# The last block product accumulated on an earlier product's PSUM bank and written out in three parts

## The chip, the cores and the metric

The kernel runs on one core of a Trainium2 chip. The metric is the device time of one execution, in microseconds. A core has a matrix engine (TensorE, PE in the profile, with its weight loads shown as PEld), two engines that can read the matrix engine's result memory PSUM (VectorE, shown as DVE, and ScalarE, shown as ACT), GpSimd (POOL), and SyncE (SP), which here mostly starts DMAs. PSUM is handed out in banks of 512 fp32 values for each of 128 partitions.

## The reference

```python
# x [8, 8, 512, 64], state [8, 8, 32, 64], w_in [512, 2048], w_out [2048, 512]
scores = scale * x @ state.T;    xread = softmax(scores) @ state      # 512 rows per batch and head
scores2 = scale * state @ x.T;   sread = softmax(scores2) @ x         # 32 rows per batch and head
x2 = concatenate([xread, sread], axis=2), heads side by side: [8 * 544, 512]
h = x2 @ w_in
g = maximum(0.01 * h, h)
out = g @ w_out                                                       # [4352, 512] float32
```

## The kernel before

The eight batches go through attention and the first product one after the other. The first product leaves the activations of a batch, already passed through the leaky ReLU, as `hT`: 2048 hidden features on partitions, 512 rows. The second product (`hT` times `w_out`) of batches 2 to 7 is done by a scheme of Strassen's kind: the batch's rows, the hidden features and the output columns are each cut in two, and seven block products take the place of eight. The block products are numbered 1 to 7. Each has 256 output rows (two groups of 128, index `i` of the bank) and `HC` = 256 output columns, so one block product fills one PSUM bank `[P, 2, HC]`, and it is a sum over `NM` = 8 slices `m`. That makes 16 matmuls of 128x128 weights by 256 columns for a block product.

The block products are done in the order 1, 2, 6, 5, 7, 3, 4 on two banks: 1, 6, 7 and 4 share one, 2, 5 and 3 the other. 6 and 7 accumulate on what 1 left, 3 on what 5 left; 1, 2, 5 and 4 start afresh. `save` copies a bank to SBUF (1, 6, 5, 7, by ScalarE), and the four quarters of the output are then made by additions: `join` (line 569, DVE: bank plus a saved copy) and one addition of two saved copies by GpSimd (line 627). In steady state product 4 is such a `join` too: bank plus `sv[7]`, the saved state of its own bank after product 7.

Batch 7 is the last, and its second product is finished after the loop, between the pieces of a smaller product for the 256 rows of `sread` (tiles `hs`, `yhs`, banks `yu`). `before.run(9)` finishes product 7 of batch 7 with its `save`, the `sread` product follows, `before.run(8)` does product 3 and its `join`, and then the last loop of the kernel does product 4. There it is written out by hand: one group `i` of 128 rows at a time. The first group goes on the bank that held 1, 6 and 7 (`before.bank[7]`, shown as `yq`), the second on a bank of its own (`yz`). DVE adds the saved copy of product 7 to each (line 1090), and `before.out` (line 594) starts one DMA of 128 KB for each, the first on ScalarE's queue, the second on SyncE's.

The order of instructions on each engine is the order in which the program issues them. The waits between engines are put in by the framework, from the tiles that the instructions read and write. All matmuls of the block products are issued at line 557, in `unit`.

Of the kernel before, what the change touches and what calls it, by code (L numbers as in the profile page):

```python
# [9 lines left out]
P = 128  # L10
# [10 lines left out]
FP32 = mybir.dt.float32  # L21
AF = mybir.ActivationFunctionType
ALU = mybir.AluOpType
# [4 lines left out]
def kernel(  # L28
# [9 lines left out]
    nc = tc.nc  # L38
# [9 lines left out]
    psum = ctx.enter_context(tc.tile_pool(name="psum", bufs=2, space=bass.MemoryType.PSUM))  # L48
# [5 lines left out]
    VEC, SCA, POO = nc.vector.tensor_copy, nc.scalar.copy, nc.gpsimd.tensor_copy  # L54
# [452 lines left out]
    HC = DM // 2  # L507
# [17 lines left out]
    class Fast:  # L525
# [19 lines left out]
            with nc.allow_low_precision(reason="operands of a product"):  # L545
                (eng or nc.vector).tensor_tensor(out=S[n][:, ms], in0=u[:, ms], in1=v[:, ms], op=op)  # L546

        def unit(self, bank, n, m, first, of=None):
            A, S = self.A, self.S
            lhs = {1: A[1, 1], 2: A[1, 2], 4: A[2, 2]}.get(n)  # L550
            if lhs is None:
                lhs = S[{3: 3, 5: 0, 6: 1, 7: 2}[n]]
            rhs = {1: B11, 2: B21, 3: B22}.get(n)
            if rhs is None:
                rhs = tw[{4: 3, 5: 0, 6: 1, 7: 2}[n]]
            for i in range(self.sub) if of is None else (of,):
                nc.tensor.matmul(  # L557
                    bank[:, i, :], lhsT=lhs[:, m, P * i:P * (i + 1)], rhs=rhs[:, m, :],
                    start=(first and m == 0 and (i == 0 or of is not None)), stop=(m == NM - 1),
                    skip_group_check=True,  # L560
                )
# [139 lines left out]
    def max0(u):  # L701
        m = att.tile([P, NG], FP32, name="m0", tag="m0")
        nc.vector.tensor_reduce(out=m[:], in_=sct[u][:], axis=AX.X, op=ALU.max, negate=True)
        return m

    def split0(m):
        hi = att.tile([P, NG], BF16, name="hi0", tag="hi0")
        VEC(hi[:], m[:])
        lo = att.tile([P, NG], BF16, name="lo0", tag="lo0")
        with nc.allow_low_precision(reason="the second of two parts of one fp32 value"):  # L710
            nc.vector.tensor_tensor(out=lo[:], in0=m[:], in1=hi[:], op=ALU.subtract)
        return hi, lo
# [53 lines left out]
    m = max0(0)  # L766
    xt0_evict(1, pxt, (SCA, VEC))
    rows0(0)
    m = split0(m)
    scores0(1)  # L770
    m = m, max0(1)
# [124 lines left out]
    for s in range(16):  # L896
# [4 lines left out]
        if s % 2:  # L901
            pb, hT, i, jq = fill[s // 2]
# [27 lines left out]
    before = None  # L930
    weights_open()
    for b in range(2, B):
# [16 lines left out]
        for s in range(16):  # L949
# [70 lines left out]
            if std:  # L1020
                i, jq = std.pop(0)
# [11 lines left out]
        before = now  # L1033
# [33 lines left out]
    for n in (1, 2, 6, 5, 7, 3, 4):  # L1067
        bank = v if n in (2, 5, 3) else u
# [6 lines left out]
        elif n == 7:  # L1075
            nc.gpsimd.tensor_tensor(
                out=ysb[1][:, :, HC:], in0=fs.sv[7][:], in1=fs.sv[5][:], op=ALU.add
# [5 lines left out]
            fs.join(ysb[1][:, :, :HC], bank, 7)  # L1083
            out_s(1)
    before.run(8)
    for i in range(2):
        bank = before.bank[7] if i == 0 else psum.tile([P, 2, HC], FP32, name="yz", tag="big", bufs=1)[:]
        for m in range(NM):
            before.f.unit(bank, 4, m, first=True, of=i)
        nc.vector.tensor_tensor(  # L1090
            out=before.yo(1)[:, i, :HC], in0=bank[:, i, :], in1=before.f.sv[7][:, i, :], op=ALU.add
        )
        before.out(1, slice(0, HC), i, eng=(nc.scalar, nc.sync)[i])


# [28 lines left out]
```

## Time and the profile before

| what | us |
|---|---|
| median of three runs (lowest, highest) | 204.59 (204.48, 204.68) |
| profiled execution, its own time | 204.49 |
| its span, first to last instruction | 202.7 |
| PE busy in it | 197.0 (97%) |
| DVE busy | 151.4 (75%) |
| ACT busy | 143.7 (71%) |
| mean granted TensorE clock | 1.000 |

The span is the profiled execution without what lies around it; here 1.8 us of the execution's time lie outside the span. The busy time of PE counts a matmul from its start to its modelled end, and consecutive matmuls overlap, so a matmul shown as 273 ns may follow its predecessor by much less. The duration of a DMA's row is its issue; its landing is given apart.

### The profile page before, as it was taken

The numbers are of one execution on the slowest core, as the hardware profiler recorded it, in microseconds if no ns is written. First come the engines' busy times: TensorE is split into PE (matmuls) and PEld (weight loads), VectorE is DVE, ScalarE is ACT, GpSimd is POOL, SyncE is SP. The second block draws the span as 40 slices with busy tenths as digits, with TensorE's granted clock in tenths as the row PEclk, the third lists the DMA queues.
The fourth block names the chain that finished last, engine by engine and source line by source line (L and its number), as shares of the span: only waits on it lengthen the run. The fifth ranks groups of instructions, "written<-read, shape, count | busy, mean of one in ns | idle before, by whom it ended". The sixth has DMA issues, their size and how long they took to land.

```text
span 202.7 us, 4755 instructions
## 1 busy us (share of the span) xinstructions
PE 197.0 (97%) x1964; PEld 126.0 (62%) x1964; DVE 151.4 (75%) x230; ACT 143.7 (71%) x265; POOL 39.7 (20%) x66
## 2 busy tenths in 40 slices
PE   7899999999999999999999999999999999999993
PEld 2543544444344567766776767766767677799882
DVE  1677679599799969976996699769968853686612
ACT  3458848589869796978697878788778856467710
POOL 8831002021005005200251040200020002004250
PEclk9999999999999999999999999999999999999999
DMA  6999996999477895537946795250017100410035
GB/s 189 223 207 277 229 298 113 141 303 245 53 175 214 114 275 109 103 125 253 118 29 181 240 127 105 103 159 5 0 57 198 27 0 32 178 55 0 3 89 170
DMA packets 39733, 27.99 MB, mean 138 GB/s; under 512 B 25312, under 2 KB 36704, under 8 KB 39712
## 3 DMA queue, kind: packets, MB, share of 16 engines
q1 hardware_dynamic: 34512, 20.88, 44.6%
q0 software_dynamic: 4912, 6.55, 15.8%
q10 hardware_dynamic: 288, 0.26, 0.6%
q8 instruction: 15, 0.25, 0.5%
q14 instruction: 6, 0.05, 0.1%
HBM read 17.30 MB, written 8.91 MB: 129 GB/s over the span
## 4 chain that ended last, share of the span: by engine, by line
PE 96%; DVE 1%; ACT 1%; issue 0%
PE yq L557 36%; PE ph L372 23%; PE py L487 10%; PE pm L351 4%; PE pyw L487 3%; PE pf L441 3%; PE yu L557 3%; PE pspin L132 3%; PE ph L804 2%; PE sc L206 1%; PE psn L318 1%; PE phw L383 1%; PE php L804 1%; DVE M L365 1%; ACT xT L666 1%; PE scn L695 0%
## 5 line engine op out<-in xcount | busy, mean ns | idle before, releaser
L377 ACT ACTIVATE hT<-ph 128x512 bf16<-128x512 f32 x108 | 63.5, 604 | 22.0 <-PE ph L372 21.4
L372 PE MATMUL ph<-aT,M 128*128 128x512 bf16 x216 | 62.3, 379 | 0.0
L557 PEld LDWEIGHTS <-su 128*128 128x128 bf16 x416 | 39.7, 98 | 14.5 <-DVE su L546 1.7
L557 PEld LDWEIGHTS <-hT 128*128 128x128 bf16 x288 | 27.7, 98 | 11.7 <-issue 1.1
L557 PE MATMUL yq<-tw_xf,su 128*128 128x256 bf16 x192 | 27.2, 273 | 0.0
L105 POOL CAST xb<-xl 128x512 bf16<-128x512 f32 (+1 forms) x21 | 14.4, 724 | 65.2 <-PE ph L372 40.6
L557 PE MATMUL yq<-w_out_bf,hT 128*128 128x256 bf16 x192 | 27.0, 273 | 0.0
L372 PEld LDWEIGHTS <-M 128*128 128x128 bf16 x216 | 21.0, 98 | 9.3 <-issue 0.8
L546 DVE TENSOR_TENSOR su<-hT 128x1024 bf16<-128x1024 bf16 x24 | 16.8, 700 | 10.5 <-ACT hT L377 10.5
L487 PE MATMUL py<-w_out_bf,hT 128*128 128x512 bf16 x96 | 24.2, 379 | 0.0
L487 PEld LDWEIGHTS <-hT 128*128 128x128 bf16 x128 | 12.1, 98 | 14.6 <-issue 0.9
L627 POOL TENSOR_TENSOR yo<-sv,sv 128x512 f32<-128x512 f32 x6 | 7.8, 1300 | 54.1 <-ACT sv L566 42.7
L569 DVE TENSOR_TENSOR yo<-yq,sv 128x512 f32<-128x512 f32 x17 | 11.6, 685 | 6.5 <-PE yq L557 6.5
L566 ACT COPY sv<-yq 128x512 f32<-128x512 f32 x24 | 13.9, 585 | 2.0 <-PE yq L557 1.4
L365 ACT CAST M<-pm 128x1024 bf16<-128x1024 f32 x13 | 13.2, 1014 | 0.9 <-PE pm L351 0.8
L557 PE MATMUL yq<-w_out_bf,su 128*128 128x256 bf16 x96 | 13.1, 273 | 0.0
L557 PE MATMUL yq<-tw_x,su 128*128 128x256 bf16 x96 | 13.1, 272 | 0.0
L557 PE MATMUL yq<-tw_x,hT 128*128 128x256 bf16 x88 | 12.1, 273 | 0.0
L274 ACT ACTIVATE e<-sc,mcols 128x512 bf16<-128x512 f32 x16 | 11.1, 696 | 0.0
L216 DVE TRANSPOSE_TENSOR_REDUCE mrow<-sc 128x32 f32<-128x1024 f32 x7 | 8.7, 1245 | 2.4 <-PE sc L206 2.4
L266 DVE TENSOR_REDUCE mcol<-sc 128x2 f32<-128x1024 f32 x8 | 9.7, 1215 | 0.0
L247 DVE STREAM_TRANSPOSE qb<-qh 128x1024 bf16<-128x1024 bf16 x7 | 8.7, 1245 | 0.2
(147 smaller groups left out, 271.3 us busy)
## 6 DMA issues: line engine op xcount, KB each, us to landing
xl<-in_x_dram SPq DMA_DIRECT2D x5, 1024.0 KB, 7.1
out_dram<-yo SPq DMA_DIRECT2D x10, 512.0 KB, 3.0
w_in_bf<-in_moe_w_in_dram POOLq DMA_DIRECT2D x4, 512.0 KB, 9.1
w_out_bf<-in_moe_w_out_dram POOLq DMA_DIRECT2D x4, 512.0 KB, 17.0
out_dram<-ysb SPq DMA_DIRECT2D x8, 256.0 KB, 5.1
xf<-in_x_dram SPq DMA_DIRECT2D x2, 512.0 KB, 4.8
x<-in_x_dram POOLq DMA_DIRECT2D x2, 512.0 KB, 13.8
xl<-in_x_dram POOLq DMA_DIRECT2D x1, 1024.0 KB, 19.8
```

What stands on the lines that cost most here:

```text
L105: copy(xs[b][:, :, h0:h1].rearrange("p t h d -> p h t d"), xl[b][:, h0:h1].rearrange("p h (t d) -> p h t d", t=NT),)
L216: nc.vector.tensor_reduce(out=m1[:], in_=flat.rearrange("p (c j) -> p c j", j=NS), axis=AX.X, op=ALU.max, apply_transpose=True,)
L266: nc.vector.tensor_reduce(out=m2[:], in_=a.sc[:], axis=AX.X, op=ALU.max, negate=True)
L274: nc.scalar.activation(out=a.e2[:, g], in_=a.sc[:, g, :], func=AF.Exp, bias=a.m2s[:, g:g + 1], scale=SCALE, accum_out=a.r2[:, g:g + 1],)
L365: copy(a.M[:, :, cols], pm[:])
L372: nc.tensor.matmul(ph[:], lhsT=a.M[:, g, P * j:P * (j + 1)], rhs=a.aT[:, g, :], start=(g == 0), stop=(g == 1),)
L377: nc.scalar.activation(out=hT[:, j, :], in_=ph[:], func=AF.Prelu, alpha=0.01)
L487: nc.tensor.matmul(y.py, lhsT=hT[:, j, P * i:P * (i + 1)], rhs=w_out_bf[:, j, :], start=(j == 0), stop=(j == 15),)
L546: (eng or nc.vector).tensor_tensor(out=S[n][:, ms], in0=u[:, ms], in1=v[:, ms], op=op)
L557: nc.tensor.matmul(bank[:, i, :], lhsT=lhs[:, m, P * i:P * (i + 1)], rhs=rhs[:, m, :], start=(first and m == 0 and (i == 0 or of is not No ...
L566: copy(t[:], bank)
L569: nc.vector.tensor_tensor(out=dst, in0=bank, in1=self.sv[n][:], op=ALU.add)
```

## The change

Product 4 now starts from what product 7 left on the bank: its matmuls no longer carry `start`, so the sum that DVE made with the saved copy of product 7 is made by accumulation in PSUM. All of product 4 goes on that one bank; the bank `yz` is gone. The product is done in three parts in place of two: the first group of 128 rows with all 256 columns, then the second group's first 128 columns, then its last 128 columns. Each part is copied to SBUF as it stands, the first and third by DVE and the second by ScalarE, and each has its own output DMA: the first on SyncE's queue, the second on ScalarE's, the third on SyncE's.

```diff
-        def unit(self, bank, n, m, first, of=None):
+        def unit(self, bank, n, m, first, of=None, cols=slice(0, HC)):
...
-                    bank[:, i, :], lhsT=lhs[:, m, P * i:P * (i + 1)], rhs=rhs[:, m, :],
+                    bank[:, i, cols], lhsT=lhs[:, m, P * i:P * (i + 1)], rhs=rhs[:, m, cols],
                     start=(first and m == 0 and (i == 0 or of is not None)), stop=(m == NM - 1),
...
     before.run(8)
-    for i in range(2):
-        bank = before.bank[7] if i == 0 else psum.tile([P, 2, HC], FP32, name="yz", tag="big", bufs=1)[:]
+
+    bank = before.bank[7]
+    for i, cols, copy, eng in (
+        (0, slice(0, HC), VEC, nc.sync),
+        (1, slice(0, HC // 2), SCA, nc.scalar),
+        (1, slice(HC // 2, HC), VEC, nc.sync),
+    ):
         for m in range(NM):
-            before.f.unit(bank, 4, m, first=True, of=i)
-        nc.vector.tensor_tensor(
-            out=before.yo(1)[:, i, :HC], in0=bank[:, i, :], in1=before.f.sv[7][:, i, :], op=ALU.add
-        )
-        before.out(1, slice(0, HC), i, eng=(nc.scalar, nc.sync)[i])
+            before.f.unit(bank, 4, m, first=False, of=i, cols=cols)
+        copy(before.yo(1)[:, i, cols], bank[:, i, cols])
+        before.out(1, cols, i, eng=eng)
```

`VEC` is `nc.vector.tensor_copy` and `SCA` is `nc.scalar.copy`.

## The prediction

> **What bounds the kernel now.** I read the page first: how busy the engines are, and the chain that ended last.
>
> ```profile
> PE 197.0 (97%) x1964; PEld 126.0 (62%) x1964; DVE 151.4 (75%) x230; ACT 143.7 (71%) x265; POOL 39.7 (20%) x66
> ...
> PE 96%; DVE 1%; ACT 1%; issue 0%
> ```
>
> PE bounds the kernel: 96% of the chain. The change touches only the last 5 us, so I read those next, in the chain in order of time. There the columns are start, length, and what; the last row's x8 are eight matmuls.
>
> ```profile
> 186.35 0.45 PE pf L441 x8
> ...
> 195.76 2.62 PE yq L557 x24
> 198.38 0.89 PE yz L557 x8
> 199.26 0.02 issue
> 199.29 0.42 DVE yo L1090
> ```
>
> To the very end PE runs with no gap: 24 matmuls in 2.62 us is 0.109 us for one of 256 columns. (The pf row gives the price for 128 columns with weights of their own: 0.45/8 = 0.056 us.) Then only one addition is left, and its output. Third, the timeline of the same stretch shows who follows whom.
>
> ```profile
> 197.34 1.04 PE L557 MATMUL yq<-tw_x,hT 128*128 128x256 bf16 x8
> 197.54 0.69 DVE L569 TENSOR_TENSOR yo<-yq,sv 128x512 f32<-128x512 f32 x1 [1.25 <-PE yq L557]
> 198.21 1.04 PE L557 MATMUL yz<-tw_x,hT 128*128 128x256 bf16 x8
> 198.26 1.84 SPq L594 DMA_DIRECT2D out_dram<-yo  x2
> 198.47 0.42 DVE L1090 TENSOR_TENSOR yo<-yq,sv 128x256 f32<-128x256 f32 x1 [0.24 <-PE yq L557]
> 198.93 0.35 ACTq L594 DMA_DIRECT2D out_dram<-yo  x1
> 199.29 0.42 DVE L1090 TENSOR_TENSOR yo<-yz,sv 128x256 f32<-128x256 f32 x1 [0.39 <-PE yz L557]
> ```
>
> What matters is the overlap: DVE reads the first half from 198.47 to 198.89, and PE writes the second half from 198.21 to 199.25. They can, because yq and yz are two tiles on two banks. The last addition ends at 199.71, SyncE's second issue starts at 199.74, and the DMA view gives its landing.
>
> ```profile
> out_dram<-yhs SPq DMA_DIRECT2D x4, 64.0 KB, 1.9
> out_dram<-yo ACTq DMA_DIRECT2D x1, 128.0 KB, 2.2
> out_dram<-yo SPq DMA_DIRECT2D x1, 128.0 KB, 1.9
> ```
>
> So the last output lands near 201.6, and the span ends at 202.7: a fixed 1.1 us that the change doesn't touch.
>
> **The change part by part.** *Matmuls.* 16 of 256 columns become 8 of 256 and 16 of 128. By the rows above that is 16 x 0.109 = 1.75 us against 8 x 0.109 + 16 x 0.056 = 1.77: nothing. Accumulating in place of starting afresh changes no matmul's duration. Product 7 on that bank ended before the sread product, 189.64 at the latest, and its saved copy is still needed by GpSimd's addition (line 627), so no work ahead of 197.34 goes or moves.
>
> The Trainium skill, "TensorE: Matmul & The Clock Gate", section "Back-to-back issue gap", gives about 81 ns for a matmul of 128 columns in a stream of weight loads and matmuls. The pf row shows 56 ns for just that, so the measurement decides; by the page the sum below would be larger by 2 x 7 x 0.025 = 0.35 us.
>
> *Additions that become copies.* From the groups by shape:
>
> ```profile
> L465 DVE COPY sf<-pf 128x512 f32<-128x512 f32 x2 | 1.4, 692 | 0.0
> L1090 DVE TENSOR_TENSOR yo<-yq,sv 128x256 f32<-128x256 f32 x1 | 0.4, 425 | 0.2 <-PE yq L557 0.2
> L566 ACT COPY sv<-yu 128x256 f32<-128x256 f32 x4 | 1.5, 372 | 2.4 <-PE yu L557 2.4
> L326 ACT CAST sr_n<-psn 128x128 bf16<-128x128 f32 x1 | 0.3, 265 | 0.7 <-PE psn L318 0.7
> L441 PE MATMUL pf<-tx,sw 128*128 128x128 bf16 x48 | 3.7, 219 | 0.0
> ```
>
> A DVE copy out of PSUM at 512 columns takes 692 ns; the addition of 512 columns (line 569, first row of that line in the timeline) takes 0.69 too. So a copy is no cheaper than the addition, and at 256 columns I take 425. From (692 - 425)/256 = 1.04 ns a column, 128 columns are 425 - 133 = 0.29 us. That last copy is shorter by 0.13 than the addition it replaces: the only gain inside the chain. ScalarE's copy of 128 columns is 0.27 by its nearest row; ScalarE has nothing else to do by then.
>
> *The bank.* This is the term that decides. Parts 2 and 3 are written to the bank from which part 1 and part 2 are being read. The trace of before has no such case to price it: every tile is read only when all its matmuls are done, and where two halves are finished apart, as here, the second has a bank of its own. The bounds are nothing, if PE may write other columns of a bank while it is read, and the whole of each copy, if the framework makes a writer of a bank wait for earlier readers of it. I take the second: the program gives waits by the tile, the tile is now one, and it is one bank. Then PE, whose order is fixed, stops twice, with nothing queued behind that could fill in: part 2 waits for DVE's copy, part 3 for ScalarE's.
>
> The Trainium skill, "PSUM — Partial Sum Buffer", section "PSUM bank collisions raise a hardware error", says that TensorE writing and another engine reading one bank on the same 32 partitions at once is an error even at other columns, and asks for a guard by bank. No run here shows a collision; the rule speaks against this change, and by it the sum is the one below.
>
> The price of a restart is read early in the trace, where PE waited for a copy: DVE's xT copy ends at 6.68 + 0.42 = 7.10 and PE starts at 7.17; ScalarE's ends at 6.97 + 0.58 = 7.55 and PE starts at 7.61. So 0.06 or a little less; I take 0.05. The longest such row, at 74.42 + 0.69 = 75.11 to 75.25, is 0.14. A part of 128 columns takes 7 x 0.056 + 0.219 = 0.61 us from its first start to its last end.
>
> The sum, in order:
> - part 1 ends at 197.34 + 1.04 = 198.38 as before; DVE copies from 198.47 to 198.90
> - PE restarts at 198.95, part 2 ends at 199.56; ScalarE starts 0.04 later (as DVE after yz: 199.25 to 199.29), 199.60 to 199.87
> - PE restarts at 199.92, part 3 ends at 200.53; DVE copies from 200.57 to 200.86
> - SyncE issues 0.03 later (as before), at 200.89, against 199.74: 1.15 later.
>
> *The outputs.* SyncE's queue now carries part 1, behind the 256 KB output, at about 198.9, and is free again long before 200.89. ScalarE's issue at 199.90 lands by 2.2 us later at 202.1, ahead of the last one. The last output is 64 KB in place of 128. The rows of 64 KB on SyncE's queue land in 1.9 in the middle, and the quickest of them in 1.6; the change also leaves the DMA engines with less beside it. I take 1.75, so 0.15 less than before. It lands at 202.64 against 201.64: **1.0 us later**. On the profiled execution's own time that is 204.49 + 1.0 = 205.49; the median stands 0.10 above that execution, so I predict **205.6**.
>
> **The rivals.** *No stops* (not slower). PE runs on: the three parts follow without a gap and part 3 ends at 198.21 + 15 x 0.056 + 0.219 = 199.27, as before; DVE's shorter copy ends at 199.60 in place of 199.71, and the smaller output lands 0.15 sooner: 0.26 less, 204.3. It decides if part 2's first matmul starts before 198.47, ahead of DVE's copy. For it: the columns don't overlap. Against it: one tile, one bank.
>
> *One stop.* Only DVE's copy holds PE: part 3 ends at 198.95 + 15 x 0.056 + 0.219 = 200.01, 0.52 sooner than in the sum, so 205.1. Only ScalarE's holds it: part 2 starts at 198.21, its copy ends at 199.14, part 3 ends at 199.80, 0.73 sooner: 204.9. Nothing in the profile parts the two stops from each other.
>
> *Dearer stops.* Each restart costs 0.14 in place of 0.05 (+0.18), and the last output takes 1.9 or even 2.1 us, as the others of its size did (+0.15 to +0.35): up to 206.1. For it: the 75.25 row. Against it: those DMAs had others beside them. Cheaper ones: a copy that starts 0.04 after PE in place of 0.09, a landing in 1.64, and a copy of 128 columns at DVE's shortest row (0.16, 128x2): 0.29 less, 205.3.
>
> **How the numbers follow.** Two stops as summed 0.72; two dearer stops 0.16; one stop 0.04; none 0.08. 0.2% (0.41 us) is about what a measurement of this kernel can tell from no change. Both cases with two stops are slower by more, and so is most of one stop. No stops at 204.3 is within it; only if its landing is also the quickest does it pass 204.18. So faster 0.04, within 0.06, slower 0.90. The range takes both cases with two stops, from 205.3 down a little for an unseen gain at 205.1, to 206.1; the rivals with fewer stops lie outside it.
>
> **What would show it.** Right: in the timeline after, the 24 matmuls of product 4 fall into three groups, with idle time of PE before the second put down to DVE and before the third to ScalarE, about 0.6 and 0.4 us; the chain's last part reads PE, DVE, PE, ACT, PE, DVE; SyncE's last issue stands near 200.9, and the span near 203.7. Wrong: matmuls of part 2 that start while DVE copies, a last issue before 199.74, 128-column matmuls spaced at 0.1, or a change anywhere before 197.3.

## The result, and the profile after

| | before | after |
|---|---|---|
| median, us (lowest, highest) | 204.58 (204.34, 205.08) | 205.60 (205.22, 206.57) |
| profiled execution, us | 204.49 | 205.48 |
| its span, us | 202.7 | 203.7 |

The changed kernel is slower: ratio 1.0058, with a 95% interval of 1.0036 to 1.0080. The timeline of the changed kernel shows the end of it (start, length, engine, line, operation; in brackets how long the engine had been idle, and what ended that).

```profile
197.47 1.04 PE L557 MATMUL yq<-tw_x,hT 128*128 128x256 bf16 x8
197.67 0.69 DVE L569 TENSOR_TENSOR yo<-yq,sv 128x512 f32<-128x512 f32 x1 [1.25 <-PE yq L557]
198.39 3.02 SPq L594 DMA_DIRECT2D out_dram<-yo  x3
198.60 0.42 DVE L1095 COPY yo<-yq 128x256 f32<-128x256 f32 x1 [0.24 <-PE yq L557]
199.08 0.61 PE L557 MATMUL yq<-tw_x,hT 128*128 128x128 bf16 x8 [0.57 <-DVE yo L1095]
...
199.72 0.27 ACT L1095 COPY yo<-yq 128x128 f32<-128x128 f32 x1 [5.17 <-PE yq L557]
200.02 0.35 ACTq L594 DMA_DIRECT2D out_dram<-yo  x1
200.04 0.61 PE L557 MATMUL yq<-tw_x,hT 128*128 128x128 bf16 x8 [0.35 <-ACT yo L1095]
...
200.75 0.29 DVE L1095 COPY yo<-yq 128x128 f32<-128x128 f32 x1 [1.73 <-PE yq L557]
```

Where PE ran through before, it now stands still twice: 0.57 us until DVE has copied the first part, 0.35 until ScalarE has copied the second. The chain in order of time tells the same as a relay: nothing in it overlaps any more.

```profile
198.60 0.44 DVE yo L1095
199.04 0.04 issue
199.08 0.62 PE yq L557 x8
199.70 0.02 issue
199.72 0.27 ACT yo L1095
200.00 0.04 issue
200.04 0.62 PE yq L557 x8
```

The outputs gave a part of it back (DMA view; the last number is us from issue to landing):

```profile
out_dram<-yo SPq DMA_DIRECT2D x1, 128.0 KB, 2.2
out_dram<-yo ACTq DMA_DIRECT2D x1, 64.0 KB, 1.7
out_dram<-yo SPq DMA_DIRECT2D x1, 64.0 KB, 1.6
```

**A measure for all that follows.** The moment at which the sread product ends differs from execution to execution: 195.5 to 196.2 us in the profiles of this study, in kernels whose matmuls are alike up to there. A part of it is already there at the first matmul of the first product's loop (line 372), at 36.3 to 36.9; in some of them up to 0.6 us more comes after that. So I measure from the end of the last sread matmul (yu) to the end of the span, and call it the tail. Before it is 6.96 us (from 195.76 to 202.71), after 7.81 (from 195.89 to 203.70): **0.86 us longer**; the differences are taken before rounding. Of that, SyncE's last issue is 1.20 later (5.18 after the sread product in place of 3.98), the landing 0.28 shorter (1.61 in place of 1.89), and the end of the span follows the landing 0.06 sooner. The rest of the difference of the two spans (0.13) lies ahead of the change.

### The profile page after: what moved, and what is told of

Same layout as the page of the kernel before. It is cut to its first block, busy times and chain, and to the rows that moved or that the text cites. A ratio compares the mean times of both kernels' runs of the same rounds, so it can differ in the third digit from the quotient of the medians.

```text
span 203.7 us, 4752 instructions
## 1 busy us (share of the span) xinstructions
PE 195.2 (96%) x1947; PEld 125.7 (62%) x1972; DVE 150.6 (74%) x230; ACT 144.1 (71%) x266; POOL 39.0 (19%) x66
## 4 chain that ended last, share of the span: by engine, by line
PE 88%; DMA 5%; POOL 2%; DVE 2%; issue 2%; ACT 0%; DVEq 0%; POOLq 0%
PE yq L557 37%; PE ph L372 21%; PE py L487 10%; DMA w_in_bf<-in_moe_w_in_dram 5%; PE pm L351 4%; PE pyw L487 3%; PE pf L441 3%; PE yu L557 3%; PE ph L804 2%; PE sc L206 1%; PE psn L318 1%; PE phw L383 1%; POOL w_in_bf L118 1%; DVE su L546 1%; DVE M L365 1%
## 5 line engine op out<-in xcount | busy, mean ns | idle before, releaser
L372 PE MATMUL ph<-aT,M 128*128 128x512 bf16 x199 | 59.7, 379 | 0.3
L105 POOL CAST xb<-xl 128x512 bf16<-128x512 f32 (+1 forms) x21 | 13.4, 681 | 63.8 <-DMA xl<-in_x_dram 39.5
L557 PE MATMUL yq<-tw_x,hT 128*128 128x256 bf16 (+1 forms) x104 | 13.3, 265 | 0.9 <-DVE yo L1095 0.6
```

The costliest lines, as they stand in the source:

```text
L105: copy(xs[b][:, :, h0:h1].rearrange("p t h d -> p h t d"), xl[b][:, h0:h1].rearrange("p h (t d) -> p h t d", t=NT),)
L372: nc.tensor.matmul(ph[:], lhsT=a.M[:, g, P * j:P * (j + 1)], rhs=a.aT[:, g, :], start=(g == 0), stop=(g == 1),)
L557: nc.tensor.matmul(bank[:, i, cols], lhsT=lhs[:, m, P * i:P * (i + 1)], rhs=rhs[:, m, cols], start=(first and m == 0 and (i == 0 or of is ...
```

## The experiments

Theory: PE must wait for whoever reads the bank that it writes next, and that is all of the loss. Rival: the cost is in the pieces themselves, that is narrow matmuls, accumulation or the third output. The loop at the end of the kernel is what the edits change. The ratios come from all executions of a kernel; tail, issue and landing from its one profiled execution.

| kernel | ratio to before, 95% | tail, us | last issue after sread | its landing |
|---|---|---|---|---|
| before | | 6.96 | 3.98 | 1.89 |
| after | 1.0036 to 1.0080 | 7.81 | 5.18 | 1.61 |
| two parts | 1.0019 to 1.0048 | 7.68 | 4.72 | 1.88 |
| copies last | 1.0004 to 1.0032 | 7.40 | 4.68 | 1.69 |
| first part early | 1.0000 to 1.0029 | 7.13 | 4.45 | 1.63 |
| own banks | 0.9983 to 1.0014 | 6.99 | 3.87 | 2.09 |
| own banks, three queues | 0.9976 to 0.9996 | 6.62 | 3.87 | 1.78 |

### Accumulation alone, in two parts

```diff
-        (0, slice(0, HC), VEC, nc.sync),
-        (1, slice(0, HC // 2), SCA, nc.scalar),
-        (1, slice(HC // 2, HC), VEC, nc.sync),
+        (0, slice(0, HC), VEC, nc.scalar),
+        (1, slice(0, HC), VEC, nc.sync),
```

> Product 4 accumulated on product 7's bank as in the changed kernel, but in two parts of 256 columns, each copied by DVE, with the outputs of before (ScalarE's queue, then SyncE's). Theory (PE must wait for a copy out of the bank that it writes next): one stop. DVE's copy of the first part ends at 198.90 on the clock of before, PE restarts at 198.95 and needs 1.04 us, DVE copies from 200.03 to 200.45, the last output lands at 202.37 in place of 201.63: 0.74 us slower than before, 205.3. Rival (the narrow matmuls and the third output cost the time, not the bank): as before, 204.6.

Measured: median 205.25 (before beside it 204.63), tail 0.72 longer than before. No narrow matmul and no third output are left, and most of the loss is. The waits of PE in this stretch are one line (us in total, times, longest):

```profile
PE yq L557 <- DVE yo L1094: 0.6, 1, 0.6
```

The tail shows what was worked out for one stop (0.74), so the rival falls for this part.

### Three parts, the second and third on banks of their own

```diff
-    bank = before.bank[7]
...
+        bank = before.bank[7] if tag is None else psum.tile([P, 2, HC], FP32, name=f"yz{tag}", tag=tag, bufs=1)[:]
         for m in range(NM):
-            before.f.unit(bank, 4, m, first=False, of=i, cols=cols)
+            before.f.unit(bank, 4, m, first=tag is not None, of=i, cols=cols)
-        copy(before.yo(1)[:, i, cols], bank[:, i, cols])
+        if tag is None:
+            VEC(before.yo(1)[:, i, cols], bank[:, i, cols])
+        else:
+            nc.vector.tensor_tensor(
+                out=before.yo(1)[:, i, cols], in0=bank[:, i, cols], in1=before.f.sv[7][:, i, cols], op=ALU.add
+            )
```

> The three parts of the changed kernel, but only the first accumulates on product 7's bank; the second and the third start afresh on a bank of their own each, and DVE adds the saved copy of product 7. Theory (the stops come from the shared bank): PE has no idle time, the third part ends at 199.27 on the clock of before, DVE's addition ends at 199.60, its 64 KB output lands 1.61 us after its issue, at 201.24 in place of 201.63: 0.4 us faster than before, 204.2. Rival (narrow matmuls and the third output cost the time): it stays near 205.6.

Measured: median 204.75, ratio 0.9999 (0.9983 to 1.0014). The stops are gone, with the same narrow matmuls and the same three outputs; the rival's 205.6 is out. In its timeline the three parts of product 4 follow each other while DVE copies:

```profile
197.40 1.04 PE L557 MATMUL yq<-tw_x,hT 128*128 128x256 bf16 x8
...
198.28 0.61 PE L557 MATMUL yzbig<-tw_x,hT 128*128 128x128 bf16 x8
...
198.53 0.42 DVE L1096 COPY yo<-yq 128x256 f32<-128x256 f32 x1 [0.24 <-PE yq L557]
198.72 0.61 PE L557 MATMUL yzsc<-tw_x,hT 128*128 128x128 bf16 x8
```

But the gain of 0.4 us that I expected isn't there. SyncE's last issue is 0.11 sooner than before, as worked out; its 64 KB landed 2.09 us later, not 1.61. That is taken up below.

### All matmuls first, the copies after them

```diff
-    for i, cols, copy, eng in (
+    parts = (
...
-    ):
+    )
+    for i, cols, copy, eng in parts:
         for m in range(NM):
             before.f.unit(bank, 4, m, first=False, of=i, cols=cols)
+    for i, cols, copy, eng in parts:
         copy(before.yo(1)[:, i, cols], bank[:, i, cols])
```

> The changed kernel with all 24 matmuls of product 4 issued first and the three copies and outputs after them, all on the one bank. Theory: PE has no idle time and ends at 199.27 on the clock of before. If readers of one bank take turns too, DVE copies until 199.74, ScalarE until 200.06, DVE until 200.41, and the last output lands at 202.05: 0.4 us slower than before, 205.0. If DVE and ScalarE may read one bank at once, DVE's second copy ends at 200.07 and the last output lands at 201.71: 0.1 us slower, 204.7. Rival (narrow matmuls and the third output): near 205.6, with PE's time of the three parts unchanged.

Measured: median 205.10, tail 0.44 longer than before; PE has no idle time. The accumulation, the narrow matmuls and the third output are all still here, and the 24 matmuls take 1.93 us, as many as before (197.34 to 199.27): none of the three costs PE anything. The copies went one after the other:

```profile
199.74 0.42 DVE L1097 COPY yo<-yq 128x256 f32<-128x256 f32 x1 [1.13 <-PE yq L557]
200.20 0.27 ACT L1097 COPY yo<-yq 128x128 f32<-128x128 f32 x1 [5.40 <-DMA out_dram<-yhs]
200.49 0.35 ACTq L594 DMA_DIRECT2D out_dram<-yo  x1
200.50 0.29 DVE L1097 COPY yo<-yq 128x128 f32<-128x128 f32 x1 [0.33 <-ACT yo L1097]
```

ScalarE starts 0.04 after DVE's end, though the line names a DMA that had long landed, and DVE's last copy waits for ScalarE's end. So the case in which readers take turns, 0.4 slower, is the one that came. They share two tiles, the PSUM tile that both read and the output tile `yo` that both write. A kernel further down, with products 3 and 4 by turns, separates the two: there DVE's last addition and ScalarE's copy before it write the same halves of `yo` as here, but read two PSUM tiles, and by the semaphores in its trace DVE waits for PE alone. Here DVE's last copy waits for ScalarE's. So the turns come with the PSUM tile. Even this, with all three copies behind the last matmul, is quicker than the changed kernel.

### The first part ahead of product 3

Product 3 uses the other bank; its `before.run(8)` moves into the loop, behind the first part.

```diff
-    before.run(8)
...
         copy(before.yo(1)[:, i, cols], bank[:, i, cols])
         before.out(1, cols, i, eng=eng)
+        if i == 0:
+            before.run(8)
```

> The changed kernel with the first part of product 4 (matmuls, copy, output) moved ahead of product 3, which works on the other bank; parts two and three stay last. Theory: DVE's copy of the first part lies beside product 3's matmuls, the stop of 0.57 us goes, that for ScalarE's copy (0.35 us) stays. Part 2 ends at 198.82 on the clock of before, part 3 at 199.79, DVE's copy at 200.19, the last output lands at 201.83: 0.2 us slower than before, 204.8. Rival: near 205.6.

Measured: median 204.99, tail 0.17 longer than before. The stop behind the first part is gone, since product 3's 1.75 us of matmuls cover DVE's copy; the other is there unchanged:

```profile
PE yq L557 <- ACT yo L1093: 0.4, 1, 0.4
```

So the two stops are separate: in the two-part kernel only the first is there, here only the second.

### Two banks in one tile

```diff
+    wide = psum.tile([P, 2, 2, HC], FP32, name="yz", tag="big", bufs=1)
...
+        bank = before.bank[7] if k is None else wide[:, k]
```

`k` is 0 for the second part and 1 for the third; the rest is the own-banks kernel.

> The second and third part start afresh in one PSUM tile of two banks, each part in a bank of its own; DVE adds the saved copy of product 7 to both. If the waits follow the bank: no idle time of PE, the span as with two tiles, 202.8. If they follow the tile: PE waits some 0.35 us before the third part, span 203.2.

Measured: one execution, 204.56 us, span 202.8.

```profile
198.82 0.29 DVE L1099 TENSOR_TENSOR yo<-yz,sv 128x128 f32<-128x128 f32 x1
199.14 0.36 ACTq L594 DMA_DIRECT2D out_dram<-yo  x1
199.16 0.61 PE L557 MATMUL yz<-tw_x,hT 128*128 128x128 bf16 x8 [0.38 <-DVE yo L1099]
```

PE waited 0.38 us, although the third part goes to another bank than the one that DVE reads, and starts afresh. So here the wait came with the tile, not with the bank, and not with the accumulation. The span doesn't show it: the last issue was later (4.41 us after sread, against 3.87 with own banks), but its output landed in 1.62 in place of 2.09.

### Where the gain of the own banks went

The own-banks kernel and, as a control, the kernel before, both with this edit in `done`:

```diff
-                self.out(0, slice(HC if self.b == B - 1 else 0, DM))
+                if self.b < B - 1:
+                    self.out(0)
```

> The kernel with the second and third part on banks of their own, with one thing left out: the 256 KB output of product 3 of the last batch is not written. Theory (the three outputs after it crowd the DMA engines, so the last one landed 2.09 us after its issue and ate the gain): it lands in 1.6 to 1.7 us, 0.4 us faster than with that output, 204.3. Rival (the landing of the last output doesn't depend on it): 204.7, and 2.1 us.

> The kernel before without the same 256 KB output of product 3 of the last batch, as a control: theory, the last output of 128 KB, which landed 1.89 us after its issue, lands in about 1.75, since only the other 128 KB output lies beside it: 0.1 us faster than before, 204.5. Rival: no change.

Measured: own banks without that output 204.25 (ratio 0.9977 to 1.0000), the last output landing in 1.67, tail 6.64; the control 204.63 (0.9995 to 1.0015), landing in 1.90, tail 7.03. So the 64 KB of the own-banks kernel were held up by what lay beside them, and the control's 128 KB were not: there my expectation of 0.1 us missed. The view by stretches shows how busy the DMA engines were. Its columns are the stretch, its length, the busy time of PE, PEld, DVE, ACT and POOL (with the instructions), the granted clock, and last the DMA engines' mean busy share and GB/s. First the own-banks kernel, then the kernel before, then the own banks without the 256 KB:

```profile
198.00:199.00 1.00, 1.00 (x18) 0.97 (x16) 0.76 (x3) 0.00 (x0) 0.00 (x0) 1.00 0.92 244
199.00:200.00 1.00, 0.33 (x6) 0.16 (x3) 0.51 (x2) 0.00 (x0) 0.00 (x0) 1.00 0.94 278
200.00:201.00 1.00, 0.00 (x0) 0.00 (x0) 0.00 (x0) 0.00 (x0) 0.00 (x0) 1.00 0.95 298
```

```profile
199.00:200.00 1.00, 0.25 (x3) 0.00 (x0) 0.42 (x1) 0.00 (x0) 0.00 (x0) 1.00 0.98 298
200.00:201.00 1.00, 0.00 (x0) 0.00 (x0) 0.00 (x0) 0.00 (x0) 0.00 (x0) 1.00 0.81 278
```

```profile
199.00:200.00 1.00, 0.65 (x12) 0.48 (x9) 0.82 (x3) 0.00 (x0) 0.00 (x0) 1.00 0.53 139
200.00:201.00 1.00, 0.00 (x0) 0.00 (x0) 0.00 (x0) 0.00 (x0) 0.00 (x0) 1.00 0.73 226
```

With own banks the DMA engines are over 0.9 busy from 198 to 201, and the last 64 KB share them with the outputs ahead. By the packets in the trace the first of these 64 KB starts 0.87 us after the issue, much as in the changed kernel (0.84), but all of them take 0.68 us in place of 0.35. The changed kernel's quick landing of 1.61 was not a merit of its small output alone: by the time its stops had let it go, the DMA engines were nearly idle (0.19 busy from 201 to 202). Why the 128 KB of the kernel before, with 0.98 and 0.81, were not held up too stays open.

### Getting the outputs out sooner

Five kernels followed from that. The first takes turns between products 3 and 4 (`C` is product 3's bank, `A` product 7's; `part` is eight matmuls):

```diff
-    before.run(8)
...
+    part(C, 3, 0, whole)
+    add(0, 0, whole, C, 6)
...
+    part(A, 4, 0, whole)
+    VEC(before.yo(1)[:, 0, :HC], A[:, 0, :])
...
+    part(C, 3, 1, whole)
+    add(0, 1, whole, C, 6)
...
+    part(A, 4, 1, left)
+    SCA(before.yo(1)[:, 1, left], A[:, 1, left])
...
+    part(last, 4, 1, right, first=True)
+    add(1, 1, right, last, 7)
```

> Products 3 and 4 done by turns on their two banks, so that each bank is read while PE writes the other: 3 first half, 4 first half (accumulated, copied), 3 second half, 4 second half left (accumulated, copied by ScalarE), 4 second half right (on a bank of its own, added by DVE). Every part has its own output, so the 512 KB of products 3 and 4 are spread over 2.5 us in place of 1.5. Theory (a bank is taken for writing only when its reader is done, and the landing of the last output depends on the outputs beside it): no idle time of PE, last issue at 199.63 on the clock of before, landing 1.6 to 1.7 us later at 201.3: 0.35 us faster than before, 204.25. Rival (a landing of 64 KB at the end takes 2.1 us whatever lies beside it): as before, 204.6.

Measured: median 205.00 (ratio 1.0016 to 1.0038), a miss. PE has no idle time and the last issue is at 3.87 after sread, as planned; but the outputs, earlier and closer to those of sread, landed 2.2 to 3.3 us after their issue, with the DMA engines 0.96 to 1.01 busy from 198 to 201, and the tail was 7.05. Its last two operations both write `yo` but read two PSUM tiles, and by its semaphores the second waited only for PE:

```profile
198.88 0.27 ACT L1108 COPY yo<-yq 128x128 f32<-128x128 f32 x1 [4.44 <-DVE yo L1088]
...
199.32 0.29 DVE L1088 TENSOR_TENSOR yo<-yz,sv 128x128 f32<-128x128 f32 x1 [0.47 <-PE yz L557]
```

A further 0.3 us lies outside its span (2.08 to 2.18 us there in every execution, against 1.72 to 1.85 in all other kernels); the cause of that stays open.

Two merge the sread outputs, by a destination of three dimensions (4 batches, 32 rows, 512 columns), the own-banks kernel and the kernel before:

```diff
-        for bb in range(4):
-            r0 = (4 * i + bb) * SROW + S
-            (nc.gpsimd, nc.sync)[i].dma_start(out[r0:r0 + NS, :], ysb[i][NS * bb:NS * (bb + 1), 0, :])
+        (nc.scalar, nc.sync)[i].dma_start(
+            out.rearrange("(b s) f -> b s f", s=SROW)[4 * i:4 * i + 4, S:, :],
+            ysb[i][:, 0, :],
+        )
```

> The three parts on banks of their own, and the eight 64 KB outputs of sread merged into two of 256 KB, one on ScalarE's queue and one on SyncE's. Theory (with the stops gone, the end is set by the DMA engines, which are busy from 197 on with outputs that were issued one after the other over 2 us): the sread outputs start together near 196.3, the DMA engines are done with them sooner, and the last 64 KB output lands 1.6 to 1.75 us after its issue at 199.65: 201.3 on the clock of before, 0.35 us faster than before, 204.2. Rival (2.1 us landing remains, since as many bytes are to be written): as before, 204.6.

> The kernel before with the same merged sread outputs and nothing else. Theory: its last 128 KB output lands in 1.75 us in place of 1.89: 0.1 us faster, 204.5. Rival (the merging alone is the gain): as fast as the other kernel with merged outputs, 204.2.

Measured: 208.53 and 208.57 us, 4 us slower, the opposite of both expectations. The stretches of the first of them:

```profile
198.00:199.00 1.00, 1.00 (x18) 0.96 (x17) 0.76 (x3) 0.00 (x0) 0.00 (x0) 1.00 0.21 45
199.00:200.00 1.00, 0.30 (x6) 0.12 (x3) 0.47 (x2) 0.00 (x0) 0.00 (x0) 1.00 0.26 92
```

With the same bytes pending the DMA engines are only 0.2 to 0.3 busy, and the outputs behind them landed 5 to 7 us after their issue (2.1 to 2.4 with the eight separate ones). The two kernels agree with and without the own banks, so it is the merging that costs it; it also moved four outputs from GpSimd's queue to ScalarE's, but three separate ones on that queue landed in 1.6 to 2.1 us (the three-queue kernel below). The packets in the trace tell more: those of the first merged output ran mostly four and never more than five at a time, from 196.8 to 201.4, and those of the second began only at 200.6. The separate outputs had up to 16 at a time. That fits a transfer spread over four of the 16 DMA engines, and four is also the first dimension of its destination; no run changes that dimension, so the reason is not shown.

The last two are the own-banks kernel with the sread outputs apart, but issued otherwise: on three queues, or by halves of the columns, each half right behind the operation that makes it.

```diff
-            (nc.gpsimd, nc.sync)[i].dma_start(...)
+            ((nc.gpsimd, nc.gpsimd, nc.scalar, nc.scalar), (nc.sync, nc.sync, nc.scalar, nc.gpsimd))[i][bb].dma_start(...)
```

> The three parts on banks of their own, and the eight 64 KB outputs of sread issued on three queues (GpSimd three, ScalarE three, SyncE two) in place of two, unmerged. Theory (the DMA engines, busy to the end, set the landing of the last output): the sread outputs are all issued some 0.6 us sooner, the engines are done sooner, and the last 64 KB output lands in 1.8 us in place of 2.1: 0.2 us faster than before, 204.3. Rival (the landing is fixed at 2.1): as before, 204.5.

```diff
-    def out_s(i):
+    def out_s(i, cols, eng):
...
             fs.join(ysb[0][:, :, :HC], bank, 1)
+            out_s(0, slice(0, HC), nc.gpsimd)
...
+            out_s(1, slice(HC, DM), nc.gpsimd)
...
-            out_s(0)
+            out_s(0, slice(HC, DM), nc.scalar)
...
-            out_s(1)
+            out_s(1, slice(0, HC), nc.sync)
```

> The three parts on banks of their own, and the sread outputs written by halves of 256 columns as soon as each half is made: the first 128 KB go out at 192, when the DMA engines are idle, the next at 195.3. Theory (the DMA engines set the landing of the last output): 128 KB less lie in the crowded stretch, the last output lands in 1.65 us in place of 2.1: 0.35 us faster than before, 204.2. Rival (the landing is fixed at 2.1, or the narrower rows cost the DMA engines as much as was moved): as before, 204.5.

Measured: three queues 204.26 against 204.51 for before beside it, ratio 0.9986 (0.9976 to 0.9996): a little faster than the kernel before, by about what was expected, though the interval barely clears 1. The last output landed in 1.78, and the DMA engines worked earlier (stretches of that kernel; in the kernel before the shares were 0.75 and 0.87):

```profile
197.00:198.00 1.00, 1.00 (x11) 0.90 (x10) 0.34 (x1) 0.00 (x0) 0.45 (x1) 1.00 0.94 295
198.00:199.00 1.00, 1.00 (x17) 0.95 (x15) 0.76 (x3) 0.00 (x0) 0.00 (x0) 1.00 0.48 139
```

Early halves gave 204.48 (ratio 0.9986 to 1.0006), no difference that can be told: its last output landed as early (5.67 us after sread, as with three queues 5.65), but the span ended 1.29 us after that landing in place of 0.97. SyncE waits for the outputs one after the other at the end, at 0.06 us for each (here at 201.54, 201.61, 201.67 and so on); in this kernel the one that landed last stands early in that row, so six more waits came after it, against one with three queues.

## Why the prediction was right

The direction and the mechanism came as forecast. The time did too (205.6), but that it agrees to the tenth is partly luck, as the last terms below show. Point by point:

- **PE at the end.** Right: the three groups of matmuls, the stops where they were put, 0.57 and 0.35 us against "about 0.6 and 0.4". The 128-column matmuls kept the 0.056 us of the pf row: a part took 0.61 us, as summed. The Trainium skill, "TensorE: Matmul & The Clock Gate", section "Back-to-back issue gap", gives about 81 ns for one; an estimate by that is 7 x 0.081 + 0.219 = 0.79 us for a part, and the trace, with 0.61, doesn't bear it out.
- **The bank.** The decisive choice between nothing and a whole copy was right. Its reason, "one tile, one bank", named two things; the kernel with two banks in one tile shows that the tile is enough to cause the wait. Whether PE could write one part of a bank while another is read was not tried: no kernel here lets a matmul run into a tile while that tile is read. The rule of the Trainium skill, "PSUM — Partial Sum Buffer", section "PSUM bank collisions raise a hardware error", that such a write and read collide is shown by no run here.
- **Copies for additions.** Right: 425, 266 and 292 ns against 425, 270 and 290.
- **The restart.** 0.05 us taken; 199.02 to 199.08 and 199.99 to 200.04 measured.
- **The last issue.** 1.15 later forecast, 1.20 measured. The missing 0.05: DVE's last copy began 0.10 after the third part's end, not 0.04. It now waits for two engines, PE and ScalarE, and the chain shows a separate step of DVE's queue ahead of it.
- **The last landing.** 1.75 forecast, 1.61 measured: the term that was mis-sized most, by 0.14, at the row's quickest end.
- **The end of the span.** Taken as a fixed 1.1 us behind the landing; 1.09 before and 1.03 after. The change did touch it: one wait of SyncE fewer comes after the last landing.
- **The total.** With these the tail is 0.86 longer, where 1.0 was forecast. The medians differ by 1.02, with room in the interval for both (0.0036 to 0.0080 of 204.6 is 0.7 to 1.6 us); so the executions can't tell the two, and the agreement to the tenth is luck.
- **The rivals.** "One stop" was not run as such; the nearest kernels came close to its prices: 205.1 worked out for DVE's stop alone with three parts, 205.25 measured with two; 204.9 for ScalarE's alone, 204.99 measured with the first part ahead of product 3. "No stops" was right in its work on PE and wrong in its time. It took the last output to land 0.15 sooner; with the stops gone it landed 0.2 later, and the kernel ended level with before, not at 204.3. The step that failed there: the landing was taken over from the case with two stops, where the DMA engines have been let run nearly idle; without the stops they are still over 0.9 busy.

## What to carry to other kernels

Splitting the last piece of work so that its end is short pays only if the pieces don't share a PSUM tile: in these kernels a matmul into a tile that is being copied out waited for the copy, and the relay PE, DVE, PE, ScalarE cost more than the shorter last step saved. Accumulating saved nothing either, since DVE's copy of 256 columns takes as long as the addition did (0.42 us). Banks of their own for the pieces took the stops away, and so did work on another bank between them, for the stop that it covered; neither alone made the kernel faster than before. So look also at the DMA engines' share near the end before counting on a shorter last step. If they are busy to the last, issuing the earlier outputs otherwise may help and may not: of the four ways tried, three queues gained a little, early halves nothing, taking turns lost 0.6 us and merging 4.

## What the runs showed of the hardware that I had not expected

- Two outputs of 256 KB with a three-dimensional destination kept the DMA engines only 0.2 to 0.3 busy from 197 to 200, with mostly four packets at a time, and made the kernel 4 us slower than eight outputs of 64 KB.
- With the sread outputs apart, the same last 64 KB took 1.61 to 2.22 us from issue to landing, by what lay beside it, while 128 KB at the end took 1.88 to 1.90 with and without 256 KB beside it.
- At the end of the kernel SyncE's waits for the outputs cost 0.06 us each, and which output lands last decides how many of them come after it: 0.97 to 1.29 us from the landing to the end in kernels that differ only in their outputs.
